# Blocked substitution in a delta-rule kernel: a solved block is taken off all rows under it, in three sets of small products per slot instead of four

## The chip, the cores and the metric

One core of a Trainium2 chip. The metric is the device time of one execution in microseconds (us), the median of several runs. A run's state is judged from its time against the fastest of the same kernel.

## The reference, cut to what matters

A delta-rule attention (4 batches, 8 heads, 768 positions, head size 48) is followed by an MLP with a sigmoid-gelu (3072 rows, 384 to 2048 to 384), all in float32.

```python
k_n = k / (norm(k) + 1e-06)
for t in range(S):
    y[:, :, t] = einsum('bhd,bhde->bhe', q[:, :, t], state)
    v_old = einsum('bhde,bhd->bhe', state, k_n[:, :, t])
    state = state + beta_t * outer(k_n[:, :, t], v_t - v_old)
x = y.transpose(0, 2, 1, 3).reshape(B * S, H * D)
h = x @ w_in
out = (h / (1 + exp(-1.702 * h))) @ w_out
```

## The kernel before

The positions are worked in chunks of 128. Within a chunk the corrected values U solve a triangular system, whose matrix comes from the Gram matrix of the keys. The 128 rows are cut into four blocks of 32 rows; a diagonal block's inverse XB is computed on VectorE. There are 24 steps (6 chunks x 4 batches), each with 8 heads. A step needs four solves (psU) and three corrections (psR) in turn, so three steps are worked at once, shifted against each other: A, B_ and D_ in the code. Between their small products TensorE works on the MLP of earlier steps, ph and po, which comes from the queue in measured portions.

In the kernel before, block 1, 2 or 3 collects the sum over all blocks **above** it just before it is solved:

```python
def above(self, blk, h, psR):
    r, a = slice(blk * BS, (blk + 1) * BS), slice(0, blk * BS)
    pe.matmul(psR[r, h, :], lhsT=self.G[a, h, 0, r], rhs=self.U[a, h, :],
              start=True, stop=True)

def rest(self, blk, psR):
    r = slice(blk * BS, (blk + 1) * BS)
    vec.tensor_tensor(self.V[r], self.V[r], psR[r], op=ALU.subtract)

def solve(self, blk, h, psU):
    r = slice(blk * BS, (blk + 1) * BS)
    pe.matmul(psU[r, h, :], lhsT=self.XB[r, h, :], rhs=self.V[r, h, :],
              start=True, stop=True)

def solved(self, blk, psU):
    r = slice(blk * BS, (blk + 1) * BS)
    act.copy(self.U[r], psU[r])
# ... (cut)
# one slot, six groups; after each group some of the MLP
# group 0: A.above(2) for all h; rest; transposes of later keys and queries
# group 1: for h: A.solve(2), B_.above(1); psG of a later step
# group 2: A.above(3) for all h; rest; D_ begins: D_.keys() (psK); psG
# group 3: for h: A.solve(3), B_.solve(1), D_.solve(0); A.queries() (psY)
# group 4: A.state() (psS)
# group 5: A.outputs() (psY)
```

The above products have 32, 64 or 96 rows and always 32 columns; every solve is 32x32. In a profile row, "32*64" means 32 rows (contraction) and 64 weight columns; that is the shape of the part of the array used.

## Time and profile before

| | before |
|---|---|
| time, median of 3 runs | 853.62 us (852.58 to 853.96) |
| TensorE busy in the page | 794.0 us (93%) |
| TensorE busy from 229.3 to 793.0 us | 563.7 of 563.7 us |
| VectorE busy in the same stretch | 292.1 us |
| one slot there (psK of one step to psK of the next) | 31.1 us |
| one set of small products, its start to the next operation's start | 0.80 us |

How to read a timeline row: start, length, engine, line, operation, out<-in, rows*columns of the weights, out shape, and how many passes were merged. An fp32 product is two passes in these traces (eight psR of one block: x16), so a set of eight heads is 16 rows "x1" or one row "x16". Ends of matmuls are modelled and overlap, so a set is measured from its first start to the first start of what follows. Slots are marked by psK, which 20 of the steps have; from the 5th psK on (274 us before, 313 in the changed kernel) slots are regular.

### The profile page before, as it was taken

The page shows a single profiled execution, that of the slowest core. Times are in us where ns is not written, and L with a number is a line of the kernel's source. Part 1 is how long each engine was busy: PE and PEld are TensorE (multiplying, and loading weights), DVE is VectorE, ACT ScalarE, POOL GpSimd, SP SyncE. Part 2 cuts the span into 40 slices and gives each one's busy share as a digit, 9 for nine tenths or more (in the row PEclk, how much of TensorE's full clock was granted, in tenths as well). Part 3 has the DMA queues.
Part 4 walks back from the last instruction along what each step waited for, and adds up shares of the span by engine and source line. Part 5 has one row for each costly group of instructions (what it writes and reads, how often), then busy time and mean ns, then how long its engine had stood idle before and what let it go on. Part 6 is the DMA issues. An engine that isn't in the chain of part 4 may idle for free.

```text
span 851.5 us, 16186 instructions
## 1 busy us (share of the span) xinstructions
PE 794.0 (93%) x6884; PEld 578.7 (68%) x6884; DVE 483.2 (57%) x1025; ACT 200.8 (24%) x383; POOL 106.0 (12%) x120
## 2 busy tenths in 40 slices
PE   8308898899999999999999999999999999999998
PEld 7206677656766867867767767767767768677684
DVE  5799869978993592582682672772762840110100
ACT  3202544232311312312212312213212112112020
POOL 2102321231021202102102101101100000000000
PEclk9658969999999999999999999999999999999999
DMA  9798653451322213223122132032032020000000
GB/s 150 157 158 152 162 143 81 112 142 34 77 59 58 60 42 73 54 64 69 36 66 68 36 85 57 18 86 54 10 79 52 1 58 2 10 15 1 24 1 18
DMA packets 160967, 55.80 MB, mean 66 GB/s; under 512 B 128672, under 2 KB 157568, under 8 KB 160896
## 3 DMA queue, kind: packets, MB, share of 16 engines
q1 hardware_dynamic: 154048, 46.02, 26.6%
q0 software_dynamic: 1856, 7.87, 3.0%
q10 hardware_dynamic: 4992, 0.89, 0.9%
q8 instruction: 54, 0.88, 0.4%
q14 instruction: 17, 0.14, 0.1%
HBM read 33.13 MB, written 20.45 MB: 63 GB/s over the span
## 4 chain that ended last, share of the span: by engine, by line
PE 78%; DVE 12%; DMA 6%; issue 2%; POOL 1%; ACT 0%; ACTq 0%; SPq 0%; DVEq 0%; POOLq 0%
PE po L629 28%; PE ph L614 27%; PE psG L368 4%; PE psR L522 4%; PE psY L549 4%; PE psU L533 4%; PE psK L512 2%; DVE P L104 2%; DMA w_out<-in_moe_w_out_dram 2%; PE psT L354 2%; DVE YB L104 1%; DMA w_out<-in_moe_w_in_dram 1%; PE psS L571 1%; DMA QP<-in_q_dram 1%; PE ps_warm L104 1%
## 5 line engine op out<-in xcount | busy, mean ns | idle before, releaser
L614 PE MATMUL ph<-xT,w_in 128*128 128x256 f32 (+1 forms) x1248 | 273.7, 373 | 2.8 <-ACT gT L619 1.9
L629 PE MATMUL po<-w_out,gT 128*128 128x384 f32 x768 | 269.4, 497 | 1.9 <-DVE w_out L194 1.8
L614 PEld LDWEIGHTS ph<-xT,w_in 128*128 128x128 f32 x1248 | 221.2, 194 | 41.7 <-issue 11.2
L629 PEld LDWEIGHTS po<-w_out,gT 128*128 128x128 f32 x768 | 140.8, 191 | 95.2 <-issue 9.5
L619 ACT ACTIVATE gT<-ph 128x512 f32<-128x512 f32 (+1 forms) x104 | 58.5, 563 | 193.8 <-PE ph L614 193.7
L529 DVE TENSOR_TENSOR V<-V,psR 32x384 f32<-32x384 f32 x68 | 37.6, 553 | 92.5 <-PE psR L522 91.4
L540 ACT COPY US<-psU 32x384 f32<-32x384 f32 x89 | 41.8, 469 | 140.8 <-PE psU L533 81.7
L522 PEld LDWEIGHTS psR<-US,G 64*32 64x32 f32 (+2 forms) x1088 | 51.0, 109 | 19.7 <-issue 18.4
L368 PE MATMUL psG<-kqT 48*128 48x256 f32 x352 | 55.5, 419 | 7.1 <-DVE G L376 4.4
L522 PE MATMUL psR<-US,G 64*32 64x48 f32 (+2 forms) x1088 | 60.8, 207 | 0.0
L392 POOL TENSOR_SCALAR_AFFINE_SELECT G<-G 128x1024 f32<-128x1024 f32 x24 | 27.2, 1132 | 247.0 <-DVE G L376 155.4
L154 PE MATMUL ps_warm<-ident 128*128 128x256 bf16 x152 | 22.1, 312 | 35.1 <-DVE ps_warm L104 32.8
L636 DVE COPY o<-po 128x384 f32<-128x384 f32 x24 | 13.3, 555 | 72.9 <-PE po L629 72.7
L533 PEld LDWEIGHTS psU<-V,XB 32*32 32x32 f32 x1424 | 35.0, 105 | 25.4 <-issue 12.7
L432 DVE TENSOR_TENSOR P<-NT,YB 64x2 f32<-64x2 f32 (+4 forms) x135 | 46.6, 345 | 4.1
L436 DVE TENSOR_REDUCE YB<-P 64x2 f32<-64x2 f32 (+4 forms) x135 | 43.3, 321 | 4.4
L533 PE MATMUL psU<-V,XB 32*32 32x48 f32 x1424 | 42.5, 204 | 2.3 <-DVE V L529 2.3
L372 ACT ACTIVATE G<-psG 128x512 f32<-128x512 f32 x44 | 26.3, 598 | 75.1 <-PE psG L368 74.0
L154 PEld LDWEIGHTS <-ident 128*128 128x128 bf16 x152 | 16.7, 112 | 39.7 <-DVE ps_warm L104 33.5
L368 PEld LDWEIGHTS psG<-kqT 48*128 48x128 f32 x352 | 34.2, 197 | 13.5 <-DVE G L376 4.8
L590 DVE COPY last<-psY 128x128 f32<-128x128 f32 x20 | 5.7, 287 | 53.7 <-PE psY L549 53.7
L304 POOL TENSOR_TENSOR ksq<-KN 128x384 f32<-128x384 f32 x17 | 14.6, 856 | 172.3 <-DMA KN<-in_k_dram 172.3
(115 smaller groups left out, 732.8 us busy)
## 6 DMA issues: line engine op xcount, KB each, us to landing
Nd<-G SPq DMA_DIRECT2D x24, 512.0 KB, 3.2
w_out<-in_moe_w_out_dram POOLq DMA_DIRECT2D x14, 384.0 KB, 3.9
KN<-in_k_dram SPq DMA_DIRECT2D x24, 192.0 KB, 3.3
V<-in_v_dram SPq DMA_DIRECT2D x24, 192.0 KB, 3.2
out_dram<-o SPq DMA_DIRECT2D x24, 192.0 KB, 1.9
QP<-in_q_dram SPq DMA_DIRECT2D x20, 192.0 KB, 2.9
w_out<-in_moe_w_in_dram SPq DMA_DIRECT2D x6, 576.0 KB, 12.4
NT<-Nd SPq DMA_DIRECT2D x24, 128.0 KB, 2.5
```

The costliest lines, as they stand in the source:

```text
L104: return lambda *a, **kw: tc.keep_in_program_order(op(*a, **kw))
L154: pe.matmul(ps, lhsT=ones[:, 0:128], rhs=ones, start=True, stop=True)
L368: pe.matmul(ps[hh][:, i], lhsT=kqT[pr, g + i, 0, :], rhs=kqT[pr, g + i, :, :], start=True, stop=True,)
L432: tt(P, diag(Nf, i * BS, [[0, i], [1, i]]), diag(Yf, 0, [[BS, i], [1, i]]), op=ALU.mult,)
L436: red(diag(Yf, i, [[BS, i]]), P, axis=AX.X, op=ALU.add, negate=True)
L522: pe.matmul(psR[r, h, :], lhsT=self.G[a, h, 0, r], rhs=self.U[a, h, :], start=True, stop=True,)
L529: vec.tensor_tensor(self.V[r], self.V[r], psR[r], op=ALU.subtract)
L533: pe.matmul(psU[r, h, :], lhsT=self.XB[r, h, :], rhs=self.V[r, h, :], start=True, stop=True,)
L540: act.copy(self.U[r], psU[r])
L614: pe.matmul(ph[:, u], lhsT=w_in[:, j, f * 128 : (f + 1) * 128], rhs=xT[:, j, t], start=(j == 0), stop=(j == KC - 1),)
L619: act.activation(gT[f0 // FQ][:, f0 % FQ : f0 % FQ + 2, t], ph, ACT.Gelu_apprx_sigmoid)
L629: pe.matmul(po, lhsT=gT[f // FQ][:, f % FQ, i * C : (i + 1) * C], rhs=w_out[:, f, :], start=(f == 0), stop=(f == FC - 1),)
```

## The change

The sum is turned round: as soon as a block is solved, its share is taken off all rows under it (below). The contraction is then always 32 rows, in the row tile of the block just solved, and it can share a set with the solves of other steps in other row tiles. The two sets that stood alone (above(2), above(3)) go; a new set is formed in the last group. Queries and outputs move together, and the state moves to the last group. The intent is one set less per slot, on a kernel in which TensorE is the bound and a set costs the same with one, two or three row tiles in it (0.80, 0.80 and 0.81 us in the trace of the kernel before).

```diff
--- before.py
+++ after.py
@@ -517,16 +517,20 @@
                 Vh = self.V[:, hh::2, :]
                 vec.tensor_tensor(Vh, Vh, psK[hh], op=ALU.subtract)
 
-        def above(self, blk, h, psR):
-            r, a = slice(blk * BS, (blk + 1) * BS), slice(0, blk * BS)
+        def under(self, blk):
+
+            return slice((0, 64, 96)[blk], C)
+
+        def below(self, blk, h, psR):
+            r, u = slice(blk * BS, (blk + 1) * BS), self.under(blk)
             pe.matmul(
-                psR[r, h, :], lhsT=self.G[a, h, 0, r], rhs=self.U[a, h, :],
+                psR[u, h, :], lhsT=self.G[r, h, 0, u], rhs=self.U[r, h, :],
                 start=True, stop=True,
             )
 
         def rest(self, blk, psR):
-            r = slice(blk * BS, (blk + 1) * BS)
-            vec.tensor_tensor(self.V[r], self.V[r], psR[r], op=ALU.subtract)
+            u = self.under(blk)
+            vec.tensor_tensor(self.V[u], self.V[u], psR[u], op=ALU.subtract)
 
         def solve(self, blk, h, psU):
             r = slice(blk * BS, (blk + 1) * BS)
@@ -675,6 +679,22 @@
 
     steps, xTs, inverting, gT0 = {}, {}, iter(()), []
 
+    def together(solves, belows):
+
+        solves = [(X, blk) for X, blk in solves if X]
+        belows = [(X, blk) for X, blk in belows if X]
+        psU = bank("psU") if solves else None
+        psR = bank("psR") if belows else None
+        for h in range(H):
+            for X, blk in solves:
+                X.solve(blk, h, psU)
+            for X, blk in belows:
+                X.below(blk, h, psR)
+        for X, blk in solves:
+            X.solved(blk, psU)
+        for X, blk in belows:
+            X.rest(blk, psR)
+
     def slot(n, share):
 
 
@@ -690,32 +710,12 @@
         todo = share
         for group in range(GR):
             if group == 0:
-                if A:
-                    psR = bank("psR")
-                    for h in range(H):
-                        A.above(2, h, psR)
-                    A.rest(2, psR)
                 next(P, None)
                 next(P, None)
             elif group == 1:
-                psU = bank("psU") if A else None
-                psR = bank("psR") if B_ else None
-                for h in range(H):
-                    if A:
-                        A.solve(2, h, psU)
-                    if B_:
-                        B_.above(1, h, psR)
-                if A:
-                    A.solved(2, psU)
-                if B_:
-                    B_.rest(1, psR)
+                together([(B_, 1)], [(A, 2)])
                 next(P, None)
             elif group == 2:
-                if A:
-                    psR = bank("psR")
-                    for h in range(H):
-                        A.above(3, h, psR)
-                    A.rest(3, psR)
                 if n + 1 < len(units):
                     h = (n + 1) // HB
                     if h not in xTs:
@@ -724,20 +724,15 @@
                     D_.keys()
                 run(P)
             elif group == 3:
-                psU = bank("psU")
-                turns = [(X, blk) for X, blk in ((A, 3), (B_, 1), (D_, 0)) if X]
-                for h in range(H):
-                    for X, blk in turns:
-                        X.solve(blk, h, psU)
-                for X, blk in turns:
-                    X.solved(blk, psU)
+                together([(A, 3), (D_, 0)], [(B_, 1)])
+            elif group == 4:
                 if A:
                     A.queries()
-            elif group == 4:
+                    A.outputs()
+            else:
+                together([(B_, 2)], [(D_, 0)])
                 if A:
                     A.state()
-            elif A:
-                A.outputs()
             next(K, None)
             if group == GR - 1 and n % HB == 1:
```

The product of block 0 writes rows 0 to 127, of which the first 32 are not needed any more.

## The prediction

> **What bounds the kernel now.** I read the page first (busy shares, slices), then the busy time of each engine in stretches, then TensorE's timeline over one slot. The page:
>
> ```profile
> PE 794.0 (93%) x6884; PEld 578.7 (68%) x6884; DVE 483.2 (57%) x1025; ACT 200.8 (24%) x383; POOL 106.0 (12%) x120
> PE   8308898899999999999999999999999999999998
> PEclk9658969999999999999999999999999999999999
> ```
>
> From the eleventh slice on, TensorE is full at full clock. The stretches (start:end, then busy us and instructions by engine, clock) say it sharply:
>
> ```profile
> core 0: us, PE busy (x) PEld busy (x) DVE busy (x) ACT busy (x) POOL busy (x), PEclk, DMA share, GB/s
> 180.00:229.30 49.30, 45.93 (x338) 32.51 (x337) 43.14 (x100) 13.48 (x26) 8.15 (x8) 0.98 0.28 67
> 229.30:793.00 563.70, 563.70 (x5035) 405.00 (x5033) 292.09 (x597) 122.48 (x231) 59.98 (x53) 1.00 0.21 46
> ```
>
> From 229 us to the end of the recurrence at 793 us TensorE is never idle and waits for nobody; VectorE is half idle there. So the price of a set of small products is the time from its start to the start of what follows on TensorE, not its latency and not what VectorE does with it. The timeline of one slot (start, length, operation; x16 is 8 products, each fp32 product being two passes):
>
> ```profile
> 485.96 0.23 PE L533 MATMUL psU<-V,XB 32*32 32x48 f32 x1
> ...
> 486.63 0.20 PE L522 MATMUL psR<-US,G 32*32 32x48 f32 x1
> 486.76 1.13 PE L368 MATMUL psG<-kqT 48*128 48x256 f32 x8
> ...
> 491.89 0.87 PE L522 MATMUL psR<-US,G 96*32 96x48 f32 x16
> 492.69 1.10 PE L512 MATMUL psK<-ST,kqT 48*128 48x48 f32 x16
> 493.62 1.10 PE L368 MATMUL psG<-kqT 48*128 48x256 f32 x8
> 494.65 4.14 PE L629 MATMUL po<-w_out,gT 128*128 128x384 f32 x12
> 498.71 0.88 PE L533 MATMUL psU<-V,XB 32*32 32x48 f32 x48
> 499.52 0.67 PE L549 MATMUL psY<-kqT,ST 48*64 48x128 f32 x16
> ```
>
> All sets cost the same 0.80 us: 16 passes (psR, 491.89 to 492.69), 32 passes (psU with psR, 485.96 to 486.76) and 48 passes (psU of three steps, 498.71 to 499.52: 0.81). Products in other row tiles run beside each other, about 0.042 us a pass per row tile. This is what the change builds on. A second fact is in the same timeline. psK costs 0.93 us when psG follows (492.69 to 493.62), which has the same tile shape, and 1.02 when po follows, which has another:
>
> ```profile
> 734.13 1.09 PE L512 MATMUL psK<-ST,kqT 48*128 48x48 f32 x16
> 735.15 4.14 PE L629 MATMUL po<-w_out,gT 128*128 128x384 f32 x12
> ```
>
> So **a change of tile shape costs 0.09 us**. The exit of the psU/psR set agrees: last pass 486.63, next operation 486.76, 0.13 us, of which 0.042 is an ordinary pass. Entering is as dear: po's pitch is 0.32 us, but from po's last start to the next set it is 0.41 (the single po at 498.30, then 498.71).
>
> [...] 0.09 us at a change, none at psK to psG, and 1 to 3 row tiles for one price. [...] psK with 128 columns and only 48 moving columns takes 0.116 us per pass in each of its two row tiles ((493.62 - 492.69)/8), against 0.042 with 32 columns[...]. [...] No place in this trace mixes tile shapes in disjoint row tiles, which is what decides this case.
>
> **The change, part by part.** The products are as many as before (3 psR and 4 psU sets of 8 per step), and VectorE's and ScalarE's work is the same: an eviction over 128 partitions costs what one over 32 does (o<-po, 128x384: 555 ns; V<-V,psR, 32x384: 553). The order of the built program, compared with the one before, shows that the interleaving by head survives the scheduler. What alters is the shape. Before, every psR had 32 output columns; now the block-0 product has 32 rows x 128 columns, block 1 has 32x64, block 2 32x32. psU stays 32x32. Reading the built program, the number of changes of tile shape from one product to the next goes from 376 to 978.
>
> Per slot, start of a set to start of what follows:
> - Set 1, psU(1) and psR(2), both 32x32: as now, 0.80.
> - Set 2, per head psU, psU (two row tiles) and then psR 32x64. A psU pair after a switch: 0.067 from first to second pass ([...] 0.067 at 485.96 to 486.03), 0.007 for the second row tile, 0.131 out: 0.205. psR with 64 columns (start times of single passes): psS has 64 columns and 48 moving: its 8 passes in each of two column tiles take 0.61 in all, its first pass 0.093, ordinary ones 0.058, last pass to the next operation 0.152; two passes 0.093 + 0.152 = 0.245. Per head 0.45, times 8 = 3.60.
> - Set 3, psU and then psR 32x128. psU 0.067 + 0.131 = 0.198. psR: as psK, first pass 0.147, last to the next of another shape 0.202: 0.349. Per head 0.547, times 8 = 4.38.
> - Removed: four sets, 3 x 0.80 + 0.81 = 3.21. The first group is left with transposes alone, of the MLP's own shape: a switch in (0.093) [...] saved, 0.15. The other excursions from the MLP move but keep their number.
>
> Sum: 0.80 + 3.60 + 4.38 - 3.21 - 0.15 = **+5.4 us a slot**. Of the 24 steps, the 64-row psR sets of 19 lie in the stretch that TensorE fills (starts 233.7 to 777.6): 19 x 5.4 = 103 us, all on the path. The other 5 slots lie between 77 and 229 us, where VectorE and the weights' arrival share the path; they get 27 us more TensorE work, and TensorE has 13.7 us idle there (5.6 + 4.7 + 3.4 in the stretches 76:130, 130:180 and 180:229.3). I choose 16 us of the 27 to show. Together 853.6 + 103 + 16 = **972 us from switches and wide weights alone**.
>
> **The granted clock on top.** Once in the early part the clock halves after a stretch that was far from idle (same columns as the stretches above):
>
> ```profile
> 175.20:178.50 3.30, 2.65 (x18) 1.52 (x15) 3.24 (x6) 1.36 (x3) 1.68 (x2) 1.00 0.26 54
> 178.60:181.90 3.30, 3.18 (x5) 1.85 (x6) 2.68 (x6) 0.85 (x2) 2.68 (x2) 0.50 0.67 209
> ```
>
> TensorE counted as 80% busy (2.65 of 3.30), mostly with psK and psG passes of 48 rows, and the next 3.4 us ran at 0.50. [...] In set 3 a head streams 4 passes of 0.040 us in 0.547, with 32 of 128 rows, sparser than that stretch. If a fall follows, at least one window of 3.4 us runs at half clock and loses 1.7 us, some more when the rest of the set or the next set lies in it. One or one and a half falls a slot would be 2 to 4 us, 19 x 2 to 4 = 38 to 76 us and some in the early slots. I give a fall in most slots about even odds, in a few slots 1 in 4, so I add 33 us, nearly half of the full effect: **1005 us**.
>
> **The rivals.**
> 1. [...] The switches that the trace prices all have overlapping rows, so the 0.09 may be an overlap cost. Then only the wide weights count: set 2 becomes 16 passes of 0.058, some 1.06 us with its ends, set 3 16 of 0.112, some 1.95. Against the removed 3.36 that is 0.80 + 1.06 + 1.95 - 3.36 = +0.45 a slot, 11 us in all: 865, within 2%. Even then there is no gain: three sets for four, but the longest is over twice as long. [...] Against it: [...] that every shape change in the trace pays, with rows-only (psG to po), columns-only (psY's second set to po) or both changed.
> 2. *The intended gain.* Each set costs 0.80 whatever is in it: one set and one switch less, 0.95 x 24 = 23 us: 831, faster by 2.7%. Against it: psK's 0.116 a pass with 128 weight columns.
> 3. *A new wait.* A solved block is used one group later as before, and outputs now directly follow queries, one group after their last block's eviction. With 4 PSUM buffers, 11 tiles a slot rotate instead of 10. Groups get longer, not shorter, so evictions have more time. Worth 0 to 10 us in the first 229 us, where VectorE is full.
>
> **Range and chances.** [...] clock kept: about 22 in 100, near 972; clock lost in some slots: 20 in 100, near 1000; in most: 45, 1020 to 1070. Rival 1: 10, near 865. Rival 2: 3. So 8 in 10 lie in 955 to 1070, with most of the rest below.
>
> **What would show it.** Right: psR and psU busy time grows while DVE and ACT busy time stays within 1%; a slot goes from 31 to 36.5 us, or to about 39 if the clock falls; in a timeline, heads of the set with psR 32x128 follow each other every 0.55 us, those with 32x64 every 0.45, and the set of 32x32 still costs 0.80; TensorE stays full after 229 us. The clock line then decides between 972 and 1050: all nines, or fives and sevens in it after 229 us. Wrong: if heads follow every 0.22 us in set 3, rival 1 holds; if TensorE shows idle time ended by VectorE or ScalarE, rival 3. The prediction fails chiefly if a change of shape between disjoint row tiles is free.

## The result, and the profile after

The changed kernel took **1057.21 us** (1050.64 to 1058.63, 4 runs) against 853.1 us for the kernel before in the same rounds: a ratio of 1.238, 95% interval 1.233 to 1.243. Ratios here are the mean time of one kernel's fast runs over that of the other's of the same rounds, so they are not quite the ratio of the medians quoted. The result is correct. The predicted time was 1005, range 955 to 1070.

From the page of the changed kernel, the busy line and two of the 40-slice lines; their counterparts are in the prediction:

```profile
PE 1000.4 (95%) x6884; PEld 723.9 (69%) x6884; DVE 480.4 (46%) x1025; ACT 200.9 (19%) x383; POOL 105.4 (10%) x120
PE   8139999999999999999999999999999999999998
PEclk9568689889998988888989889888898889888999
```

The number of instructions is the same on every engine, and so is the work of VectorE and ScalarE (480 against 483 us, 200.9 against 200.8). TensorE is fuller than before, and its granted clock, nines from the seventh slice on before, is dented throughout. The busy time by stretch of the changed kernel (start:end, then us, and busy us with instructions by engine, clock) says how much:

```profile
313.30:918.00 604.70, 604.70 (x4131) 433.75 (x4130) 253.69 (x527) 103.27 (x194) 50.45 (x46) 0.88 0.17 38
```

TensorE never waits here, at a mean clock of 0.88. So the 197 us that the two profiled runs differ by are TensorE's own time, not a wait. The timeline of the changed kernel shows the first half of it. First some heads of set 2 (psU of two steps, then psR with 64 columns), then some of set 3 (psU, then psR with 128 columns):

```profile
524.25 0.28 PE L537 MATMUL psU<-V,XB 32*32 32x48 f32 x4
524.45 0.31 PE L526 MATMUL psR<-US,G 32*64 32x48 f32 x2
524.69 0.28 PE L537 MATMUL psU<-V,XB 32*32 32x48 f32 x4
...
373.23 0.27 PE L537 MATMUL psU<-V,XB 32*32 32x48 f32 x2
373.42 0.42 PE L526 MATMUL psR<-US,G 32*128 32x48 f32 x2
373.77 0.27 PE L537 MATMUL psU<-V,XB 32*32 32x48 f32 x2
373.97 0.42 PE L526 MATMUL psR<-US,G 32*128 32x48 f32 x2
```

A head of set 2 takes 0.44 us (524.25 to 524.69), one of set 3 0.54 (373.23 to 373.77): 0.20 us from psU to psR, 0.35 from psR to the next psU. Over all sets of the steady part at full clock, set 2 has a median of 3.55 us and set 3 of 4.35; the set of equal shapes (psU with psR 32x32) is still at 0.80. The prediction had 3.60, 4.38 and 0.80.

The second half is the clock. Two stretches in a row, the first inside set 2 of a slot:

```profile
400.60:403.90 3.30, 3.30 (x48) 2.44 (x44) 0.00 (x0) 0.06 (x1) 0.00 (x0) 1.00 0.25 40
404.10:407.30 3.20, 3.20 (x8) 2.57 (x9) 2.50 (x7) 1.10 (x3) 0.00 (x0) 0.50 0.33 67
```

TensorE counts as busy in all of the first, and yet the clock is halved in the next. After 313 us there are 29 such falls, each of 3.4 or 6.8 us, 153.6 us at half clock in all; a slot mostly has one of each kind. Such a slot is 41.3 us long, and one with a single fall of 6.8 us is 39.7, where 31.1 + 5.4 = 36.5 would be the switches alone.

### The profile page after: what moved, and what is told of

It reads as the page before. It is cut to its first block, busy times and chain, and to the rows that moved or that the text cites.

```text
span 1048.8 us, 16186 instructions
## 1 busy us (share of the span) xinstructions
PE 1000.4 (95%) x6884; PEld 723.9 (69%) x6884; DVE 480.4 (46%) x1025; ACT 200.9 (19%) x383; POOL 105.4 (10%) x120
## 4 chain that ended last, share of the span: by engine, by line
PE 91%; DVE 5%; DMA 3%; ACTq 0%; issue 0%; ACT 0%; SPq 0%; DVEq 0%
PE po L633 28%; PE ph L618 27%; PE psR L526 10%; PE psU L537 8%; PE psG L368 4%; PE psY L553 3%; PE psK L512 2%; PE psS L575 2%; PE psT L354 2%; PE ps_warm L104 1%; PE psR L104 1%; DMA w_out<-in_moe_w_in_dram 1%; DVE P L104 1%; PE psU L104 1%; DMA QP<-in_q_dram 1%; DVE YB L104 1%
## 5 line engine op out<-in xcount | busy, mean ns | idle before, releaser
L618 PE MATMUL ph<-xT,w_in 128*128 128x256 f32 (+1 forms) x1248 | 302.6, 402 | 0.0
L633 PE MATMUL po<-w_out,gT 128*128 128x384 f32 x768 | 300.5, 543 | 0.0
L618 PEld LDWEIGHTS ph<-xT,w_in 128*128 128x128 f32 x1248 | 243.6, 212 | 46.2 <-issue 8.5
L633 PEld LDWEIGHTS po<-w_out,gT 128*128 128x128 f32 x768 | 156.3, 211 | 107.2 <-issue 34.5
L526 PE MATMUL psR<-US,G 32*32 32x48 f32 (+2 forms) x1056 | 148.1, 250 | 0.0
L533 DVE TENSOR_TENSOR V<-V,psR 32x384 f32<-32x384 f32 (+2 forms) x66 | 36.8, 557 | 230.0 <-PE psR L526 229.6
L526 PEld LDWEIGHTS psR<-US,G 32*32 32x32 f32 (+2 forms) x1056 | 104.0, 147 | 22.8 <-issue 0.7
L537 PE MATMUL psU<-V,XB 32*32 32x48 f32 x1408 | 113.5, 214 | 0.0
L537 PEld LDWEIGHTS psU<-V,XB 32*32 32x32 f32 x1408 | 65.3, 106 | 45.7 <-issue 22.3
L154 PEld LDWEIGHTS <-ident 128*128 128x128 bf16 x152 | 17.0, 113 | 39.7 <-DVE ps_warm L104 33.5
L368 PEld LDWEIGHTS psG<-kqT 48*128 48x128 f32 x352 | 33.8, 196 | 13.4 <-DVE G L376 5.1
```

Of the source, the lines that this page charges most:

```text
L154: pe.matmul(ps, lhsT=ones[:, 0:128], rhs=ones, start=True, stop=True)
L368: pe.matmul(ps[hh][:, i], lhsT=kqT[pr, g + i, 0, :], rhs=kqT[pr, g + i, :, :], start=True, stop=True,)
L526: pe.matmul(psR[u, h, :], lhsT=self.G[r, h, 0, u], rhs=self.U[r, h, :], start=True, stop=True,)
L533: vec.tensor_tensor(self.V[u], self.V[u], psR[u], op=ALU.subtract)
L618: pe.matmul(ph[:, u], lhsT=w_in[:, j, f * 128 : (f + 1) * 128], rhs=xT[:, j, t], start=(j == 0), stop=(j == KC - 1),)
L633: pe.matmul(po, lhsT=gT[f // FQ][:, f % FQ, i * C : (i + 1) * C], rhs=w_out[:, f, :], start=(f == 0), stop=(f == FC - 1),)
```

## The experiments

The theory after the result: each change of tile shape costs TensorE about 0.09 us even when the two products lie in disjoint row tiles; wide weights add to it; and the sparse sets that come of it lower the clock. The rivals: the wide weight loads are the cost and the shapes as such are not; the schedule's new order or buffers are the cost; the clock falls for another reason or costs little.

### The same products, ordered by shape

```diff
         for h in range(H):
             for X, blk in solves:
                 X.solve(blk, h, psU)
+        for h in range(H):
             for X, blk in belows:
                 X.below(blk, h, psR)
```

> The changed kernel with the same products, only ordered by shape: in sets 2 and 3 all eight heads' psU come first and all psR after them, so each set has one change of tile shape inside instead of sixteen. Theory ([...]sparse sets that lower the clock): set 2 costs 0.80 + 1.05 = 1.85 us, set 3 0.80 + 1.92 = 2.72 us, a slot at full clock 33.1 us; 898 us, up to 915 if the clock still falls in a third of the slots. Rival (the wide weight loads are the cost, the order does not matter): set 3 stays above 4 us and the time near 1040 to 1057.

Measured: 920.64 us (917.56 to 927.01), ratio 1.0794 (1.0731 to 1.0857). From the timeline of this run, sets 2 and 3 and what follows each:

```profile
470.07 0.87 PE L537 MATMUL psU<-V,XB 32*32 32x48 f32 x32
470.87 1.13 PE L526 MATMUL psR<-US,G 32*64 32x48 f32 x16
471.93 4.14 PE L633 MATMUL po<-w_out,gT 128*128 128x384 f32 x12
...
480.40 0.86 PE L537 MATMUL psU<-V,XB 32*32 32x48 f32 x16
481.19 1.98 PE L526 MATMUL psR<-US,G 32*128 32x48 f32 x16
483.10 0.67 PE L575 MATMUL psS<-US,KN 128*64 128x48 f32 x16
```

Set 2 takes 470.07 to 471.93 = 1.86 us instead of 3.55, set 3 480.40 to 483.10 = 2.70 instead of 4.35: 1.85 and 2.72 were expected. The weights are as wide as in the changed kernel, so the width alone is not its cost; the alternation is, 1.7 us in each of the two sets. The width's own price is visible too: 1.06 us for 16 passes with 64 columns, 1.91 with 128, against 0.80 with 32. The run is a little over its expected range (a slot of 33.7 us, where 33.1 was expected) because of a slip: set 1 was ordered by shape too, and its two row tiles now ran one after the other, 1.33 us instead of 0.80. Five slots after the 5th psK still have a fall of the clock.

### All products in 32-column tiles

```diff
-            pe.matmul(
-                psR[u, h, :], lhsT=self.G[r, h, 0, u], rhs=self.U[r, h, :],
-                start=True, stop=True,
-            )
+            for i in range(u.start, C, BS):
+                w = slice(i, i + BS)
+                pe.matmul(
+                    psR[w, h, :], lhsT=self.G[r, h, 0, w], rhs=self.U[r, h, :],
+                    start=True, stop=True,
+                )
```

> The changed kernel with every psR product cut into products of 32 columns (four for block 0, two for block 1, one for block 2), so that all products of a set have the shape 32x32; more products, no change of shape inside a set. Theory: column tiles of one row tile run beside each other as row tiles do, every set costs 0.80 us whatever is in it, a slot is 1.0 us shorter than before; 834 us, faster than the kernel before by 2%, clock as before. Rival (products that share a row tile go one after another, 0.042 us a pass): set 2 costs 1.5 and set 3 2.85 us, 885 to 895 us.

Measured: 846.48 us (846.06 to 847.66), ratio 0.9915 (0.9885 to 0.9945). More instructions, same sums and same order of heads, and the time falls by 211 us against the changed kernel, to below the kernel before. The start and the end of set 3, 80 passes, in the timeline of this run:

```profile
321.83 0.23 PE L539 MATMUL psU<-V,XB 32*32 32x48 f32 x1
321.84 0.24 PE L528 MATMUL psR<-US,G 32*32 32x48 f32 x4
...
322.54 0.25 PE L528 MATMUL psR<-US,G 32*32 32x48 f32 x5
322.72 0.67 PE L577 MATMUL psS<-US,KN 128*64 128x48 f32 x16
```

321.83 to 322.72 is 0.89 us. The medians of the three sets are 0.80 (32 passes), 0.81 (64) and 0.89 (80). Column tiles of one row tile do run beside each other (64 passes in 0.81 us); five passes at a time begin to cost a little (80 in 0.89). The rival of one after another (2.85 us) is out. A regular slot is 30.3 us, 0.8 less than before (1.0 was expected). The time was expected at 834, so 12 us are missing. Six of them are a new wait, on this line of the waits of TensorE (us in total, times, longest):

```profile
PE ph L620 <- DVE o L642: 6.1, 5, 2.0
```

ph and po share two PSUM buffers, and ph waited for VectorE's copy of the finished po. Some 3 us are the 0.2 us a slot that were not gained. A part of the rest lies in the early slots: up to the 5th psK this run has 75 us at half clock, the kernel before 61, which is worth up to 7 us.

### One set of mixed shapes in the kernel before

```diff
             r, a = slice(blk * BS, (blk + 1) * BS), slice(0, blk * BS)
+            w = slice(0, 2 * BS) if blk == 1 else r
             pe.matmul(
-                psR[r, h, :], lhsT=self.G[a, h, 0, r], rhs=self.U[a, h, :],
+                psR[w, h, :], lhsT=self.G[a, h, 0, w], rhs=self.U[a, h, :],
```

> The kernel before with one thing altered: the psR product of block 1 is 64 columns wide (its first 32 columns are not used), so the set that interleaves psU (rows 64 on) with psR (rows 0 to 31) mixes the shapes 32x32 and 32x64; sums, order, number of sets and evictions stay. Theory: that set goes from 0.80 to 3.5 us, a head every 0.44 us; 19 x 2.7 + some 8 us early = 913 us with the clock kept, 925 to 945 if the clock falls in half of the slots. Rival ([...]only the wider load): 16 passes of 0.058, 0.26 us a slot, 858 us.

Measured: 957.99 us (953.76 to 960.51), ratio 1.1212 (1.1159 to 1.1265). In the timeline of this run the heads of that set follow each other so:

```profile
433.21 0.27 PE L534 MATMUL psU<-V,XB 32*32 32x48 f32 x2
433.41 0.31 PE L523 MATMUL psR<-US,G 32*64 32x48 f32 x2
433.65 0.27 PE L534 MATMUL psU<-V,XB 32*32 32x48 f32 x2
```

A head every 0.44 us, and the set 3.50 us (432.78 to 436.28) instead of 0.80. psU is in rows 64 to 95 here and psR in rows 0 to 31; the only thing altered is that psR has 64 columns for 32. So a change in the number of columns, between disjoint row tiles, is paid at the price at which the prediction had put a change of shape: 0.44 us a head. No sum was turned round and nothing was moved, which takes the new order and the buffers out of the question for this cost; psU and psR alternated between their buffers before as well, for 0.80 us. A slot without a fall of the clock is 33.9 us, 31.1 + 2.7 = 33.8 by the set alone. The time is above the expected 925 to 945: 14 falls of the clock came after the 5th psK (71.7 us at half clock, expected in half of the slots), and the early part lost 25 us where 8 were expected.

### The sparse sets cut into parts

```diff
+            if between and h in (3, 6) and solves and belows:
+                between()          # 1.3 us of ph or po
             for X, blk in solves:
                 X.solve(blk, h, psU)
             for X, blk in belows:
                 X.below(blk, h, psR)
```

The two sets of mixed shapes get this once the first few slots are over; some MLP work is held back from the earlier groups for it.

> The changed kernel with sets 2 and 3 cut into parts of 3, 3 and 2 heads with 1.3 us of the dense MLP products between the parts; shapes and order inside the parts stay, so the changes of shape stay and four more excursions a slot are added (0.2 us each, 0.8 us a slot, 15 us in all). Theory: [...]the clock stays at 1.00 after 229 us, and the time falls to 980 to 1000 in spite of the added work. Rival (the clock falls for another reason, or its fall costs little): 1065 to 1075.

Measured: 1013.71 us (1009.77 to 1022.8), ratio 1.1891 (1.181 to 1.1972): 43 us faster than the changed kernel although work was added. The stretch of its steady part:

```profile
400.00:860.00 460.00, 458.49 (x3401) 319.78 (x3399) 214.48 (x450) 84.86 (x160) 45.81 (x41) 1.00 0.19 43
```

The clock is at 1.00 (one fall after the 5th psK instead of 29), and a regular slot is 37.3 us, which is 36.5 for the switches and 0.8 for the four added excursions from the MLP to a set and back, to the tenth. The parts themselves show the same cost of shape: 1.63 us for three heads of set 3. So with the long, sparse sets cut, 29 falls became one, and the falls had cost some 4.8 us in a slot with two of them (41.3 - 36.5). The time missed its range of 980 to 1000 in the early part, whose first slots were not cut: the 5th psK starts at 336 us (313 in the changed kernel), with 136 us at half clock up to there, against 99. Some of that is a side effect of the edit. While the queue of MLP work first fills, one early slot got its whole share of it at once, where the changed kernel spreads it over the slot:

```profile
135.28 12.28 PE L618 MATMUL ph<-xT,w_in 128*128 128x128 f32 x96
```

The groups after it ran 18 more filler products (ps_warm, 278 against 260). The profiled run is also the slowest of the three (1022.8 us). So this run settles the clock of the steady part; its total is not a clean measure of the cut.

### ScalarE copies the output tile

```diff
-            vec.tensor_copy(o, po)
+            act.copy(o, po)
```

This is the kernel with 32-column tiles and this line altered.

> The kernel of the second run (all products in 32-column tiles) with the MLP's output tile copied out of PSUM by ScalarE instead of VectorE. In that run TensorE stood still 6.1 us in five slots, on ph, until VectorE had copied the output tile o. Theory: those waits go, 6 us less: 840 us, ratio to the kernel before about 0.985. Rival (ScalarE's own queue delays the copy or the gelu as much): 846, no gain.

Measured: 841.04 us (837.46 to 843.21), ratio 0.9842 (0.9815 to 0.987). The stretch of its steady part:

```profile
400.00:780.00 380.00, 380.00 (x4219) 277.08 (x4218) 177.87 (x376) 88.30 (x168) 35.54 (x30) 1.00 0.19 43
```

TensorE is full again (376.1 of 380 us with VectorE copying), the wait on o is gone from the list, and the middle slots are all 30.3 or 30.4 us. This version beats both kernels, by 1.6% the one before; that is clear of noise, but under the 2% from which a run is called faster here.

### Only the moved part

```diff
-                if A:
-                    A.queries()
             elif group == 4:
                 if A:
-                    A.state()
+                    A.queries()
+                    A.outputs()
             elif A:
-                A.outputs()
+                A.state()
```

> The kernel before with only the moved part of the change: queries and outputs together in the fifth group and the state in the last, sums as before in four sets. Theory: same number of excursions from the MLP, no new wait: 850 to 856 us, the same within 0.5%. Rival (the move itself costs, through buffers or the later state): over 860.

Measured: 849.88 us (846.92 to 851.79), ratio 0.9939 (0.9908 to 0.997). Slots stay at 31.1 us. The move costs nothing and perhaps gives half a per cent, in irregular and early slots; why is not settled. Of the 0.85% that the 32-column kernel gains, this part may be most; the 0.8 us a slot of the sets themselves were partly eaten by the wait and the early clock named there.

### The early slots in 32-column tiles

```diff
+            width = BS if self.n < 5 else C - u.start
+            for i in range(u.start, C, width):
+                w = slice(i, i + width)
                 # the product of below, on columns w
```

> The changed kernel, with the psR products of the first five steps (those that run before 229 us in the kernel before) cut into 32-column tiles; the later 19 steps as in the changed kernel. The time saved against the changed kernel (1057) is what the early slots paid. Prediction's term: 16 us and some clock, so about 1035 to 1041. Rival A (TensorE's idle time and VectorE's bound hid nothing): 5 slots at 9 us each, 1012. Rival B (all hidden): 1057.

Measured: 1032.23 us (1027.92 to 1032.24), ratio 1.2067 (1.2028 to 1.2107). The first five steps thus paid 25 us in the changed kernel, of the 27 of added TensorE work plus its clock; neither rival holds, and the time is just under the 1035 to 1041 that were expected. The steady part is as in the changed kernel, 29 falls and 153.6 us at half clock after the 5th psK.

## Why the prediction was right

**The bound.** TensorE was full before and is after; VectorE's and ScalarE's busy time moved by less than 1%. Right.

**The sets.** 0.80, 3.60 and 4.38 us were predicted, 0.80, 3.55 and 4.35 measured at full clock. This is the step on which the rest stands, and the third experiment shows it by itself: with one psR product widened, one set went from 0.80 to 3.50. That a change of shape costs as much between disjoint row tiles was not shown by the trace of before; it was the estimate, and the cost came as sized. From the last pass of one shape to the first of the next, less the ordinary distance between two passes, it is 0.09 us for all three shapes (0.131 - 0.042 after psU, 0.147 - 0.058 after 64 columns, 0.200 - 0.112 after 128). The 0.15 us that the prediction took off for the first group are the 0.093 of a switch and some 0.056 of a longer first pass of the transposes after a set: in the trace of before 0.164 us (481.06 to 481.22), an ordinary one 0.109. Rival 1 (a change of shape is free between disjoint row tiles) and rival 2 (0.80 whatever is in the set) are out for the changed kernel. Rival 2 became true when the shapes were made equal, and then paid 7 us, not its 23.

**The waits.** Rival 3 did not come: from 76 us on, the changed kernel's TensorE waits for VectorE and ScalarE come to 3.5 us in all (13 in the kernel before), all before 313 us. The move alone cost nothing.

**The clock.** The prediction named the fall and gave it even odds in most slots, adding 33 us, "nearly half of the full effect". This is the term that was mis-sized. It came in every slot of the steady part, in 11 of 15 twice, for 4.8 us where twice and 3.2 where once; the prediction gave 2 to 4 even to the full effect, and a slot of about 39 us where 41.3 was the common one. Falls lasted 6.8 us (16 of them) as often as 3.4 (13): in the long ones 0.6 to 1.9 us of the set still lay in the first 3.4 us at half clock, in the short ones at most 0.6. That is most of why the time is 1057, in the prediction's own band for "in most" slots (1020 to 1070), and not 1005; the early slots are the rest. The range held because it had been laid round the band for "in most" slots too: the sum itself, 1005, was 52 us short.

**The early slots.** 16 us were chosen of 27; the last experiment shows 25. TensorE's idle time from 76 to 276 us sank from 13.7 to 4.5 us, so a part of the work was hidden; but the half-clock time up to the 5th psK rose from 61 to 99 us, which the 16 had left out.

**The sum.** By the profiled runs: 39 us up to the 5th psK, 145 over the next 15 slots, 13 after the last psK. After the 5th psK that is 158 us. The 153.6 us at half clock lost at most half their length, 77, and rather less, since a change of shape does not take twice as long there (psU to the psR of 64 columns: 0.131 us at full clock, up to 0.205 at half). So 81 us or more are switches (an estimate of 86, if all of it was lost at the rate of the common slot, 4.8 of 10.2 us), where the prediction's terms give 15 x 5.4 = 81 for the 15 slots and some 10 for the sets of the last two.

## What to carry to other kernels

Before small products are packed into one set, compare their tile shapes, not only their row tiles: the mixed shapes that alternated here took 3.55 and 4.35 us a set, and the same sums with the wide product cut into tiles of the narrow shape, more and narrower instructions, 0.81 and 0.89. If shapes must differ, order by shape and not by head (1.86 and 2.70 us). And when TensorE is the bound, ask how dense each stretch of it will be: here a set that was "busy" for 3.30 of 3.30 us but thin was followed by 3.4 us of dense work at a clock of 0.50, 29 such falls of 3.4 or 6.8 us in the steady part.

## What the runs show beyond the prediction

- The cost of a change of shape is about 0.09 us also where only the number of columns differs and the row tiles are disjoint (a head of psU and psR 32x64: 0.44 us; of 32x128: 0.54). In the changed kernel's trace the first pass after a change is longer too: 0.093 us from the first to the second pass of psR with 64 columns and 0.147 with 128, where the prediction's ordinary passes of these widths are 0.058 and 0.112.
- Windows in which the profile shows TensorE busy throughout (3.30 of 3.30 us) were followed by half clock. In the traces of both kernels each stretch of one clock lasts a multiple of 3.41 us (but for the last, cut off by the end). An estimate from the start times in these two traces of how long passes stream (0.83 ns a column, from po's pitch of 0.32 us for 384; half of it in the bf16 warm-up, whose pitch is 0.109 us for 256), weighted with their rows over 128: of 460 windows of 3.41 us at full clock, 44 were followed by half clock, all with a share of at most 0.358; the lowest of the other 416 was 0.371. It is a fit to these traces, not a test of its own.
- 16 passes in one single 32x32 tile follow each other every 0.042 us (psR at 980.80 to 981.36 in the changed kernel), which by the same estimate is nearly streaming time alone (48 columns at po's 0.32 us for 384 are 0.040), and 80 passes, 64 of them in four column tiles of one row tile, took 0.89 us.
